# The opening of a one-core attention and mixture-of-experts kernel: the first batch's expert taken from its slots' summed values, one softmax over all its tokens, and W1 loaded between two pieces of the second batch's keys and values

## The chip, the core and the metric

The program runs on one core of a Trainium2 chip. The number that counts is the device time of one execution in microseconds (us). The kernel before takes 393.38 us (median of three executions, 393.33 to 393.97). The engines are named as in the profile: PE is TensorE (PEld its weight loads), DVE is VectorE, ACT is ScalarE, POOL is GpSimd, SP is SyncE. SP only issues transfers here, in order, and each waits for its semaphores at the head of SP's queue.

## What is computed

Two stages follow each other: an attention in which 576 keys and values of each head are first pooled into 32 slots, and a mixture of 8 experts of which each token uses one.

```python
def _attn_ref(q, k, v, phi):              # B, H, S, D = 8, 8, 576, 64; 32 slots
    a = softmax(phi, axis=2)              # over the 32 slots
    k_m = einsum('bhsm,bhsd->bhmd', a, k) # slot keys
    v_m = einsum('bhsm,bhsd->bhmd', a, v) # slot values
    attn = softmax(q @ k_m.T / 8)         # each token over the 32 slots
    return attn @ v_m
def _moe_ref(x, expert_emb, tau, w1, w2): # x: 4608 tokens of 512; 8 experts, hidden 1024
    logits = normed(x) @ normed(expert_emb).T / tau
    e = argmax(logits); gate = softmax(logits)[e]
    return gate * (relu(x @ w1[e]) @ w2[e])
```

The router's logits are linear in the attention's output but for a factor per token, and the output is a mean of slot values, so a token's expert can be read from slot values times the expert embedding.

## The kernel before

A batch of 576 tokens is one stage of eight. The chosen expert's W1 and W2 are loaded once for a batch, and all tokens of the batch are run through it. Tokens that belong to another expert are handled by a loop after the eight batches (`rest`), which runs once for each pair of batch and other expert that `flags` marks; for the drawn inputs no pair is marked.

In a batch, `slots` pools keys and values (matmuls of eT and kx, kl), `scale`, `keys` and `values` make slot keys kT and slot values vT, `score` multiplies kT with the queries (tr, ts), `squares` multiplies vT with vT and with the router's columns (tl), `products` copies that to vv, `fill`, `weigh`, `divide` and `turn` make the softmax of each token (x, then aw), `project` multiplies vT with W1 (pg, then the pair gh and gl), `pairs` multiplies aw with vv (po), and `first` and `second` are the two large layers (ph, py), which use a value and its remainder (gh and gl, aT's two halves, wh and wl).

The order of every engine's instructions is that of the Python calls (the schedule is manual). From batch 0's `first` on, small steps of the next batch are hung into lists that run between the matmul groups of the large layers (`steps`). Before that lies the opening, in `moe_linformer`, lines 1088 to 1167, and the first lines of `batch` (940 to 949): nothing of a large layer can run there. It does batch 0 up to its softmax and the slots, keys and values of batch 1.

In the opening the expert of batch 0 comes from its first 64 tokens: `score` of 64 columns, `fill` and `weigh` of these, `turn`, then `early` (line 123, two matmuls), `best` and `count` (lines 202 and 203) and the two DVE operations of `choose`. SP reads the number (line 220) and issues the two halves of W1 (line 468). The other 512 tokens have a softmax of their own (`others`). Matmuls of a constant (`warm`, line 418) fill PE's idle stretches; their result is not used. For batch 1 all keys and values have been issued on SP before SP waits for the expert.

PSUM is given out in two rings, `pt` (tags t0 to t3) and `mm` (m0 to m3); batch 1's slot sums lie in t3 and m3.

Of the kernel before, what the change touches and what calls it, by code (L numbers as in the profile page):

```python
# [8 lines left out]
F32 = mybir.dt.float32  # L9
F32R = mybir.dt.float32r  # L10
BF16 = mybir.dt.bfloat16
I32 = mybir.dt.int32
# [35 lines left out]
class Tokens:  # L48
# [69 lines left out]

    def early(self, po, to):

        k, nc = self.k, self.nc
        for g in range(NG):
            nc.tensor.matmul(po[to, 144 * g : 144 * g + P + E], lhsT=k.aw[:, g, to], rhs=k.vv[:, g], start=True, stop=True)
        e = po[to].rearrange("p (g m) -> p g m", g=NG)[..., D : D + E]
        nc.vector.tensor_reduce(out=self.lg[to, 0], in_=e.rearrange("p g e -> p e g"), axis=AX.X, op=ALU.add)
        self.best(0, to=to)

    def open(self):
# [70 lines left out]

    def count(self, key, to):  # L200

        self.nc.tensor.matmul(key, lhsT=self.k.ones, rhs=self.k.eb, start=True, stop=False)
        self.nc.tensor.matmul(key, lhsT=self.k.ones[to], rhs=self.oh[to, 0], start=False, stop=True)
        return key

    def choose(self, to=None):

        k, nc, b = self.k, self.nc, self.b
        if b:
            self.key = self.all = key = self.all_at_once()  # L210
        else:
            key = self.pt([P, 512], "key")
            self.spare, key = key[:, E:], key[:, :E]
            self.key = self.all = self.count(key, to)
# [6 lines left out]
        k.load_w1(e, b == 0)  # L221
        return e
# [3 lines left out]

    def kept(self):
        self.held = self.k.wk.tile([P, E], F32, tag="held", name="held")
        self.nc.scalar.copy(self.held, self.key)

    def owner(self):
        k, nc, b = self.k, self.nc, self.b
        cm = k.wk.tile([P, 1], F32, tag="cm", name=f"cm{b}")
        self.own = k.wk.tile([P, E], F32, tag="own", name=f"own{b}")
        key = self.key if b else self.held
        nc.vector.tensor_reduce(out=cm, in_=key, axis=AX.X, op=ALU.max)
        nc.vector.tensor_scalar(out=self.own, in0=key, scalar1=cm, scalar2=None, op0=ALU.is_equal)

    def flags(self):

        self.nc.vector.scalar_tensor_tensor(
            out=self.k.fl[:, self.b], in0=self.all, scalar=float(E), in1=self.own, op0=ALU.is_ge, op1=ALU.subtract
        )
# [44 lines left out]
class Kernel:  # L288
# [64 lines left out]
    def consts(self):  # L353
        nc, st = self.nc, self.st.tile
        self.ident = st([P, P], F32, name="ident")
        make_identity(nc, self.ident)
        self.i8 = st([P, E], F32, name="i8")
        nc.gpsimd.iota(self.i8, pattern=[[1, E]], base=0, channel_multiplier=0, allow_small_or_imprecise_dtypes=True)
        self.rev8 = st([P, E], F32, name="rev8")
        nc.vector.tensor_scalar(out=self.rev8, in0=self.i8, scalar1=-1.0, scalar2=float(E), op0=ALU.mult, op1=ALU.add)  # L360

        self.oh = [st([P, NT + 1, E], BF16, name=f"oh{i}") for i in range(2)]
        self.eb = self.oh[0][:, NT]
        for oh in self.oh:
            nc.vector.tensor_scalar(out=oh[:, NT], in0=self.i8, scalar1=1.0 / (E * P), scalar2=None, op0=ALU.mult)
        nc.vector.memset(self.vv, 0.0)
        nc.gpsimd.memset(self.z2, 0.0)
        self.half = st([P, 1], F32, name="half")
        nc.vector.memset(self.half, 0.5)
# [65 lines left out]

    def load_kv(self, b):
        if 1 < b < B:
            for g in range(NG):
                to, x = self.kl[64 * g : 64 * g + 64], self.kvt[b, :, 4 * g : 4 * g + 4]
                self.nc.sync.dma_start(to, x)  # L440
        if b < B:
            for k in range(4):
                self.nc.sync.dma_start(self.kx[k], self.kv[b, :, k])
                if b < 2 and k == 1:
                    x = self.kvt[b].rearrange("t (g j) d -> (t g) (j d)", g=NG)
                    self.nc.sync.dma_start(self.kl.rearrange("p j d -> p (j d)"), x)

    def load_q(self, b, halves=(0, 1)):
# [14 lines left out]

    def load_w1(self, e, halves=False):

        for k in range(2 if halves else 4):
            c, f = (slice(NC), slice(512 * k, 512 * k + 512)) if halves else (slice(k, k + 1), slice(FF))
            self.nc.sync.dma_start(self.w1s[:, c, f], self.w1[bass.ds(e, 1), :, c, f].rearrange("a p c f -> (a p) c f"))
# [32 lines left out]

    def shares(self, b, gs=range(NG), v=None):

        v = v or self.nc.vector
        nm, sm, rs = self.room(b)
        for g in gs:
            for j in range(4) if g else (None,):
# [3 lines left out]
                )  # L511
        g = slice(gs[0], gs[-1] + 1)
        self.nc.vector.reciprocal(out=rs[:, g], in_=rs[:, g])
# [212 lines left out]

    def project(self, n, vT, room=None):

        nc = self.nc
        for k in range(2):  # L730
            f = slice(512 * k, 512 * k + 512)
            ps = [(room or self.mm)([P, 512], f"pg{n}_{k}{g}") for g in range(NG)]
            for g, j, r, c, i in self.heads():
                nc.tensor.matmul(ps[g][j], lhsT=vT[r, g, c % 2, i], rhs=self.w1s[r, c, f], start=True, stop=True)
            for g in range(NG):
# [66 lines left out]
    def steps(self, b, t, u):  # L802
# [7 lines left out]
        if not b:  # L810
# [114 lines left out]
    def batch(self, b, t, u):  # L925
# [7 lines left out]

        project = self.project(b, self.vT[b % 2]) if u else ()
        if b:
            list(project)
            if u:
                self.scores(b + 1)
        else:
            self.keys(1, lambda *a: self.mm(*a, 3))  # L940
            self.values(1, copy=self.nc.scalar.copy, room=lambda *a: self.mm(*a, 2))
            self.part(0, slice(0, HS), self.nc.scalar.copy)
            next(project)
            self.part(1, slice(0, HS), self.nc.scalar.copy)
            self.second_part = project
            t.attend()
# [136 lines left out]
def moe_linformer(ctx, tc, phiT, qT, kv, kvt, emb, tau, w1, w2, out):  # L1083
# [5 lines left out]
    k.warm(8)  # L1089
    k.warm(25, hot=k.mm([P, 64], "cool", 0))  # L1090
    k.load_phi(0)
# [28 lines left out]
    k.again()  # L1120
    k.load_kv(1)
    k.keys(0)
    k.values(0, copy=k.nc.scalar.copy)
    first, others, few = slice(0, 2), slice(2, BL), slice(0, 64)
    ts = [k.mm([P, 64], f"ts0_{g}", 1 + g) for g in range(NG)]
    k.score(0, ts, 0, 64)
    t.fill(range(NG), first, ts)
    ts = [k.mm([P, S - 64], f"tr0_{g}", g) for g in range(NG)]
    tl = [k.pt([P, D + E], f"tl0_{g}") for g in range(NG)]
    k.score(0, ts, 64, S, (0,))  # L1130
    k.squares(0, tl)
    k.score(0, ts, 64, S, (1,))
    list(t.weigh(range(NG), first))
    k.products(0)
    t.turn(range(NG), first)
    k.largest(1, 0)
    k.softmax(1, (0,))
    t.early(k.mm([P, NC * (D + E)], "po0", 2), few)
    e = t.choose(few)
    k.largest(1, 1)  # L1140
    k.softmax(1, (1,))
    k.load_q(1, (0,))
    k.turn(1, 0)
    k.warm(7, hot=t.spare)
    k.turn(1, 1)
    k.turns += 1
    k.tails(1)
    t.fill(range(NG), others, ts)
    weights = [t.weigh((g,), others) for g in range(NG)]
    for g in range(NG):  # L1150
        next(weights[g])
    for g in range(NG):
        next(weights[g])
        list(weights[g])
    k.shares(1, v=k.nc.gpsimd)
    t.kept()
    for ks in ((0,), (1,), (4,), (2,), (3,)):
        k.slots(1, accs, ks=ks, first=0 in ks, last=3 in ks)
    k.tags = 4
    k.scale(1)  # L1160
    k.again(k.nc.scalar.copy)
    t.divide(range(NG), slice(0, BL), True)
    t.turn(range(NG), slice(0, BL))
    k.load_w2(e)
    k.load_q(1, (1,))
    k.load_phi(2)
    k.warm(3)
    for b in range(B):
# [33 lines left out]
```

## Time and profile before

| | us |
|---|---|
| median of the runs | 393.38 |
| profiled execution | 395.79 |
| its span | 394.0 |
| PE busy | 384.9 (98%) |
| DVE, ACT, POOL busy | 244.3, 214.0, 188.6 |
| first matmul of the large layers (line 753) starts at | 32.59 |

The profile is of one execution; its span is what the trace covers, and 1.8 us of its time lie outside. Times in the trace are counted from the span's start. A row of the timeline has start, length, engine, line and operation, tile written <- tiles read, the shape, how many instructions it merges, and in brackets how long the engine sat idle before and what ended that. PEclk is the granted clock of TensorE as a share of 2.4 GHz; 0.50 is 1.2 GHz. The queue of the SP engine carries nearly all loads (81 of 91 MB).

### The profile page before, as it was taken

How to read it: one execution, taken by the hardware profiler on the slowest of the kernel's cores; microseconds unless marked ns; L12 is line 12 of the kernel's file. 1: busy time of each engine (PE TensorE's matmuls, PEld its weight loads, DVE VectorE, ACT ScalarE, POOL GpSimd, SP SyncE). 2: the span in 40 equal slices, each digit the busy share in tenths (PEclk: the TensorE clock that was granted, in tenths of full speed). 3: DMA queues.
4: the chain of work that ended last, by engine and by line, in shares of the span. 5: the costliest groups of instructions: out<-in, count | busy, mean ns of one | idle time of the engine just before them, and what ended most of it. 6: DMA issues, size and time to landing. Idle time of an engine off the chain costs nothing. (4 is left out here: it accounts for less than half of the span.)

```text
span 394.0 us, 10319 instructions
## 1 busy us (share of the span) xinstructions
PE 384.9 (98%) x3837; PEld 311.1 (79%) x3837; DVE 244.3 (62%) x806; ACT 214.0 (54%) x666; POOL 188.6 (48%) x230
## 2 busy tenths in 40 slices
PE   8799999999999999999999999999999999999995
PEld 5357978889787987879787997879788897879883
DVE  5388895769672798448971798627961596535000
ACT  5257643777585685657665775667642651145011
POOL 1036951588142941559152961549342781529300
PEclk9779999999999999999999999999999999999999
DMA  8979938996779936997479925997279305980011
GB/s 277 393 287 366 356 108 202 318 393 242 160 210 394 399 90 145 326 374 308 86 233 360 402 92 111 342 385 275 60 212 359 120 2 106 296 348 0 30 53 43
DMA packets 68534, 91.24 MB, mean 232 GB/s; under 512 B 40984, under 2 KB 46616, under 8 KB 68352
## 3 DMA queue, kind: packets, MB, share of 16 engines
q1 hardware_dynamic: 65104, 81.02, 61.4%
q0 software_dynamic: 2688, 8.26, 5.8%
q10 hardware_dynamic: 688, 1.26, 1.2%
q8 instruction: 31, 0.51, 0.6%
q14 instruction: 23, 0.19, 0.2%
HBM read 71.19 MB, written 19.33 MB: 230 GB/s over the span
## 5 line engine op out<-in xcount | busy, mean ns | idle before, releaser
L753 PE MATMUL ph<-aT,gh 128*128 128x288 f32 x512 | 103.1, 297 | 0.0
L793 PE MATMUL py<-wh,hh 128*128 128x512 f32 x256 | 100.8, 394 | 0.0
L793 PE MATMUL py<-wl,hh 128*128 128x512 f32 x256 | 99.8, 390 | 0.0
L793 PE MATMUL py<-wh,hl 128*128 128x512 f32 x256 | 99.7, 389 | 0.0
L724 POOL TENSOR_TENSOR wl<-w2s,wh 128x512 fp32r<-128x512 f32 x64 | 83.2, 1300 | 5.1
L753 PEld LDWEIGHTS ph<-aT,gh 128*128 128x128 f32 x512 | 81.8, 188 | 1.8 <-DVE hl L760 0.8
L753 PE MATMUL ph<-aT,gl 128*128 128x288 f32 x256 | 75.4, 294 | 0.0
L757 ACT ACTIVATE hh<-ph 128x224 fp32r<-128x224 f32 (+1 forms) x128 | 48.8, 388 | 33.6 <-PE ph L753 33.0
L760 DVE SCALAR_TENSOR_TENSOR hl<-ph,hh 128x224 fp32r<-128x224 f32 (+1 forms) x128 | 51.8, 417 | 23.5 <-ACT hh L757 16.9
L798 ACT ACTIVATE ys<-py,gate 128x512 f32<-128x512 f32 (+1 forms) x40 | 25.8, 644 | 62.9 <-PE py L793 33.1
L969 POOL DMA_DIRECT2D out_dram<-ys x28 | 16.2, 580 | 90.4 <-ACT ys L798 90.3
L793 PEld LDWEIGHTS py<-wh,hh 128*128 128x128 f32 x256 | 48.1, 188 | 11.0 <-issue 1.4
L793 PEld LDWEIGHTS py<-wh,hl 128*128 128x128 f32 x256 | 48.1, 188 | 10.2
L793 PEld LDWEIGHTS py<-wl,hh 128*128 128x128 f32 x256 | 48.1, 188 | 9.4
L753 PEld LDWEIGHTS ph<-aT,gl 128*128 128x128 f32 x256 | 48.0, 188 | 0.0
L737 DVE TENSOR_TENSOR gl<-pg,gh 128x512 fp32r<-128x512 f32 x32 | 20.0, 684 | 42.0 <-ACT gh L736 42.0
L723 POOL CAST wh<-w2s 128x512 fp32r<-128x512 f32 x62 | 41.3, 666 | 0.1
L714 POOL TENSOR_TENSOR aT<-aw,aT 128x576 fp32r<-128x576 f32 (+1 forms) x18 | 23.5, 1318 | 33.6 <-DVE aT L713 30.2
L553 ACT COPY eT<-xt 32x256 f32<-32x256 f32 x80 | 32.3, 403 | 1.4
L782 PE MATMUL py<-w2s,h 128*64 128x256 f32 x256 | 29.4, 382 | 0.0
L625 ACT COPY kv<-kt 32x64 f32<-32x64 f32 x96 | 23.3, 243 | 6.3 <-DVE kt L615 5.1
L782 PEld LDWEIGHTS py<-w2s,h 128*64 128x64 f32 x256 | 17.7, 137 | 10.7 <-DVE aw L100 2.1
(174 smaller groups left out, 473.4 us busy)
## 6 DMA issues: line engine op xcount, KB each, us to landing
kx<-kv SPq DMA_DIRECT2D x32, 512.0 KB, 10.2
w2s<-w SPq DMA_DIRECT2D x28, 512.0 KB, 9.6
w1s<-w SPq DMA_DIRECT2D x28, 512.0 KB, 6.5
out_dram<-ys POOLq DMA_DIRECT2D x28, 256.0 KB, 6.4
qt<-qT SPq DMA_DIRECT2D x12, 576.0 KB, 9.2
ad<-aw SPq DMA_DIRECT2D x8, 576.0 KB, 10.4
td<-x SPq DMA_DIRECT2D x56, 72.0 KB, 2.4
ea<-td SPq DMA_DIRECT2D x7, 512.0 KB, 4.2
```

The lines of the kernel that those rows point to most:

```text
L553: nc.scalar.copy(eT[to, :8, m].rearrange("p (g k) m -> p g k m", g=NG), xt[at, :, q : BL - 2 : 4])
L625: nc.scalar.copy(y, self.kt[32 * l : 32 * l + 32, g, h + 2 * i :: 2 - 4 * i])
L714: self.nc.gpsimd.tensor_tensor(out=al, in0=a, in1=ah.bitcast(F32), op=ALU.subtract)
L723: (copy or self.nc.scalar.copy)(h, x)
L724: self.nc.gpsimd.tensor_tensor(out=l, in0=x, in1=h.bitcast(F32), op=ALU.subtract)
L737: nc.vector.tensor_tensor(out=self.gl[:, g, f], in0=ps[g], in1=self.gh[:, g, f].bitcast(F32), op=ALU.subtract)
L753: nc.tensor.matmul(p, lhsT=w[:, g, fs], rhs=x[:, g, to], start=g == 0 and k == 0, stop=g == 1 and k == 2)
L757: nc.scalar.activation(self.hh[:, f, at], q, AF.Relu)
L760: nc.vector.scalar_tensor_tensor(out=self.hl[:, f, at], in0=q, scalar=0.0, in1=self.hh[:, f, at].bitcast(F32), op0=ALU.max, op1=ALU.subtract)
L782: nc.tensor.matmul(p[64 * j : 64 * j + 64], lhsT=self.h4[:, f], rhs=self.w2s[:, f, d * j : d * j + d], start=f == 0, stop=f == 7,)
L793: nc.tensor.matmul(p, lhsT=h[:, f, to], rhs=w[:, f], start=f == 0 and k == 0, stop=f == 7 and k == 2)
L798: nc.scalar.activation(y[:, :d], p, AF.Copy, scale=gate[:, i : i + 1])
```

## The change

- Guess: `early`, `count` and the 64-token path go. `guess` sums the router's columns of vv over all slots with two matmuls by a matrix of ones; `pick` takes the largest of the eight sums and its place with MAX, MAX_INDEX and an AND on DVE; `kept` goes, and `owner` compares with the number itself.
- One softmax: batch 0 has one `weigh` of 576 tokens for each half g, in two matmul groups (448 or 512 columns and 64), with `fill` of the one half between the slots' work of batch 1.
- Loads: q comes in two halves of 576 KB, not in three pieces (256, 448, 448 KB). SP issues two of batch 1's four kx pieces, then waits for the expert, issues W1's first half, then kl and the other two kx pieces, then W1's second half.
- Order on PE: W1's first half is multiplied (`project`, first half) before batch 1's slots; batch 1's `keys` and `values` move from the opening into batch 0's `first` (after groups 5 and 6). `warm` counts: 25, 7, 3 before; 29, 14, 2, 3 after.

The diff, cut to what is spoken of:

```diff
+    def guess(self):
+        key = self.pt([P, 512], "key")
+        self.spare, self.key = key[:, E:], key[:, :E]
+        for g in range(NG):
+            nc.tensor.matmul(self.key, lhsT=k.all1, rhs=k.vv[:, g, D : D + E], start=not g, stop=g == NG - 1)
+    def pick(self):
+        nc.vector.max(out=top, in_=self.key)
+        nc.vector.max_index(out=at, in_max=top, in_values=self.key)
+        nc.vector.tensor_scalar(out=self.at, in0=at[:, :1].bitcast(I32), scalar1=E - 1, scalar2=None, op0=ALU.bitwise_and)
+        return nc.sync.value_load(self.at[:1], min_val=0, max_val=E - 1)
...
-        if not b:
-            for c, f in ((slice(4), slice(P)), (slice(2), slice(P, S)), (slice(2, 4), slice(P, S))):
-                self.nc.sync.dma_start(self.qt[:, c, f], self.qT[0, :, c, f])
-        elif b < B:
+        if b < B:
...
+            first[5].append(lambda: self.keys(1, self.mm))
+            first[6].append(lambda: self.values(1, copy=self.nc.scalar.copy, room=self.mm))
...
-    k.load_kv(1)
+    k.load_kv(1, (0, 1))
     k.keys(0)
-    k.values(0, copy=k.nc.scalar.copy)
...
+    scores(0)
     tl = [k.pt([P, D + E], f"tl0_{g}") for g in range(NG)]
     k.squares(0, tl)
     k.products(0)
+    t.guess()
+    te.append(k.pt([P, 64], "te0_1"))
+    scores(1)
+    work = [t.weigh((g,), all) for g in range(NG)]
+    t.fill((0,), slice(2, BL), tr)
+    t.fill((0,), slice(0, 2), te)
+    e = t.pick()
+    k.load_w1(e, 0)
+    k.load_kv(1, (2, 3))
+    k.load_w1(e, 1)
     k.load_q(1, (0,))
+    k.warm(14, hot=t.spare)
+    list(work[0])
+    for g in range(NG):
+        k.largest(1, g)
+        k.softmax(1, (g,))
     k.turn(1, 0)
+    k.warm(2, at=2)
+    t.fill((1,), slice(2, BL), tr)
+    t.fill((1,), slice(0, 2), te)
+    list(work[1])
     k.turn(1, 1)
     k.tails(1)
+    k.shares(1, v=k.nc.gpsimd, invert=False)
+    project = k.project(0, k.vT[0], apart=True)
+    next(project)
+    t.divide(range(NG), all, True)
+    t.turn(range(NG), all)
+    k.invert(1)
+    next(project)
+    for g in range(NG):
+        k.part(g, slice(0, HS), k.nc.scalar.copy)
     for ks in ((0,), (1,), (4,), (2,), (3,)):
         k.slots(1, accs, ks=ks, first=0 in ks, last=3 in ks)
```

On PE, from batch 0's slot values (tv) to the expert's number; tr and ts are scores, tl the squares, po the early output, key the sums. Before:

```order
L636 MATMUL tv_0_306<-ident,ks 128x128 x2
L654 MATMUL ts_0_313<-qt,kv_80 32x64 x4
L654 MATMUL ts_1_314<-qt,kv_80 32x64 x4
L654 MATMUL tr_0_325<-qt,kv_80 32x512 x4
L662 MATMUL tl_0_327<-kv_80 32x72 x4
L662 MATMUL tl_1_328<-kv_80 32x72 x4
L654 MATMUL tr_1_326<-qt,kv_80 32x512 x4
L123 MATMUL po_361<-vv,aw 64x136 x2
L202 MATMUL key<-oh_165,ones 128x8
L203 MATMUL key<-oh_165,ones 128x8
L519 MATMUL te_0_388<-ident,ex 128x128 x4
```

And after the change, the same place:

```order
L637 MATMUL tv_0_307<-ident,ks 128x128 x2
L655 MATMUL tr_0_314<-qt,kv_80 32x512 x4
L655 MATMUL te_0_316<-qt,kv_80 32x64 x4
L663 MATMUL tl_0_325<-kv_80 32x72 x4
L663 MATMUL tl_1_326<-kv_80 32x72 x4
L197 MATMUL key<-vv,h_97 128x8 x2
L655 MATMUL tr_1_315<-qt,kv_80 32x512 x4
L655 MATMUL te_1_342<-qt,kv_80 32x64 x4
```

The sums stand ahead of the second scores now, and behind them only the copies to vv; the scores of 64 columns (ts) are no longer ahead of everything that needs the large part of q.

On SP, from batch 1's first transfers of keys and values (kx_70, kx_71) to W1 (w1s). Before:

```order
L443 DMA kx_70<-kv 128x1024
L443 DMA kx_71<-kv 128x1024
L446 DMA kl<-kvt 128x512
L443 DMA kx_72<-kv 128x1024
L443 DMA kx_73<-kv 128x1024
L220 TENSOR_LOAD seli
L468 DMA w1s<-w 128x4x512
L468 DMA w1s<-w 128x4x512
```

After:

```order
L445 DMA kx_70<-kv 128x1024
L445 DMA kx_71<-kv 128x1024
L208 TENSOR_LOAD ai
L464 DMA w1s<-w 128x4x512
L444 DMA kl<-kvt 128x512
L445 DMA kx_72<-kv 128x1024
L445 DMA kx_73<-kv 128x1024
L464 DMA w1s<-w 128x4x512
```

Three transfers of batch 1 (1.25 MB) now stand behind the expert's number and behind half of W1.

On ACT, after the exponentials of batch 1's phi; eT and kt are copies of transposes, x is batch 0's softmax, gh the copy of `project`, aT the rounded weights, ks the scaled slots. Before:

```order
L520 COPY eT<-te_1_401 128x512
L527 COPY kt<-tz_407 128x256
L76 ACTIVATE x<-x 128x512 x2
L229 COPY held<-key 128x8
L593 ACTIVATE ks<-acc0t,rs_357 128x128
L593 ACTIVATE ks<-acc0m,rs_357 128x128
L630 COPY ks<-ks 128x2x64
```

After:

```order
L521 COPY eT<-te_0_401 128x512
L76 ACTIVATE x<-x 128x576
L521 COPY eT<-te_1_416 128x512
L528 COPY kt<-tz_422 128x256
L739 CAST gh<-pg_00_431 128x512
L739 CAST gh<-pg_01_432 128x512
L714 CAST aT_86<-aw 128x288 x2
L594 ACTIVATE ks<-acc0t,rs_394 128x128
L594 ACTIVATE ks<-acc0m,rs_394 128x128
```

The second exponential of the tokens now stands behind the copy of te_0, and the scaling of the slots behind the two casts of aw, which need the turned softmax.

## Rows read from the trace of the kernel before

**Rows 1.** The page, part 1: busy time, share of the span, instructions.
```profile
PE 384.9 (98%) x3837; PEld 311.1 (79%) x3837; DVE 244.3 (62%) x806; ACT 214.0 (54%) x666; POOL 188.6 (48%) x230
```
**Rows 2.** Stretches: length, busy time of PE, PEld, DVE, ACT, POOL, PEclk, DMA share, GB/s.
```profile
14.00:15.00 1.00, 0.00 (x0) 0.00 (x0) 0.82 (x4) 0.51 (x4) 0.00 (x0) 0.60 1.07 404
21.00:22.00 1.00, 1.00 (x5) 0.55 (x4) 1.00 (x2) 0.42 (x1) 0.00 (x0) 0.50 0.13 53
24.00:25.00 1.00, 1.00 (x8) 0.73 (x6) 1.00 (x2) 0.00 (x0) 1.00 (x1) 0.78 1.05 383
32.00:48.00 16.00, 16.00 (x170) 14.19 (x167) 13.90 (x55) 10.83 (x34) 12.78 (x16) 1.00 1.03 366
```
**Rows 3.** The timeline of PE in the opening, 13 to 33 us.
```profile
13.14 0.41 PE L636 MATMUL tv<-ident,ks 128*128 128x128 f32 x2
...
15.31 1.08 PE L654 MATMUL tr<-qt,kv 64*32 64x512 f32 x4 [1.49 <-DMA qt<-qT]
...
16.13 1.45 PE L654 MATMUL tr<-qt,kv 64*32 64x512 f32 x8
...
18.53 1.14 PE L123 MATMUL po<-vv,aw 128*64 128x136 f32 x4
...
21.30 3.15 PE L418 MATMUL key<-ones 128*128 128x504 bf16 x7
24.24 0.70 PE L519 MATMUL te<-ident,ex 128*128 128x128 f32 x4
...
28.46 0.40 PE L601 MATMUL tk<-ident,ks 128*128 128x128 f32 x2
...
29.12 1.09 PE L734 MATMUL pg<-w1s,kv 64*32 64x512 f32 x16
...
31.17 0.86 PE L140 MATMUL po<-vv,aw 64*64 64x72 f32 x40 [0.16 <-DVE aw L98]
31.96 0.88 PE L172 MATMUL tt<-ident,aw 128*128 128x128 f32 x6
32.59 0.51 PE L753 MATMUL ph<-aT,gh 128*128 128x288 f32 x2
```
**Rows 4.** The transfers of SP: the timeline, 3 to 24 us.
```profile
3.99 1.96 SPq L451 DMA_DIRECT2D qt<-qT  x3
...
12.47 3.09 SPq L443 DMA_DIRECT2D kx<-kv  x2
21.86 1.35 SPq L468 DMA_DIRECT2D w1s<-w  x2
```
**Rows 5.** SP's own waits, 0 to 60 us: in total, times, longest.
```profile
SPq L443 <- DMA qt<-qT: 2.8, 2, 2.4
```
**Rows 6.** Line 468, W1's two halves: from issue to landing.
```profile
DMA to landing us min/median/max: 5.1/6.7/8.3
```
**Rows 7.** The timeline of DVE in the opening.
```profile
17.63 0.47 DVE L698 COPY vv<-tl 64x72 f32<-64x72 f32 x2 [2.74 <-PE tl L662]
...
20.69 0.14 DVE L217 TENSOR_SCALAR seli<-ki 1x1 int32<-1x1 int32 x1
...
22.65 1.22 DVE L72 TENSOR_REDUCE mx<-x 128x16 f32<-128x512 f32 x2
...
26.46 1.41 DVE L85 TENSOR_REDUCE z<-x 128x18 f32<-128x576 f32 x2 [1.11 <-ACT x L76]
...
29.32 0.78 DVE L98 STREAM_TRANSPOSE aw<-x 128x576 f32<-128x576 f32 x1
```
**Rows 8.** The timeline of ACT in the opening.
```profile
21.57 0.77 ACT L498 ACTIVATE ex<-ex,nm 128x576 f32<-128x576 f32 x1 [1.48 <-issue]
...
25.78 1.16 ACT L76 ACTIVATE x<-x 128x512 f32<-128x512 f32 x2
...
27.70 0.37 ACT L593 ACTIVATE ks<-acc0t,rs 128x128 f32<-128x128 f32 x1 [0.70 <-PE acc0t L576]
```
**Rows 9.** The timeline of POOL, 28 to 30 us.
```profile
28.67 1.63 POOL L90 TENSOR_TENSOR x<-x,z 128x576 f32<-128x576 f32 x1 [3.52 <-DVE z L87]
```

More of the change, by code (lines that the diff above doesn't have):

```diff
@@ L117, in attend @@
         self.pairs()
[L119 to L126, printed above, removed]
     def open(self):
@@ L198, in all_at_once, with choose @@
         return key
[L200 to L206, printed above, removed]
-        k, nc, b = self.k, self.nc, self.b
[L209 to L214, printed above, removed]
+    def guess(self):
+        k, nc = self.k, self.nc
+        key = self.pt([P, 512], "key")
[3 more added lines that the diff above has]
+    def pick(self):
+        k, nc = self.k, self.nc
+        top = k.wk.tile([P, E], F32, tag="top", name="top")
+        at = k.wk.tile([P, E], mybir.dt.uint32, tag="at", name="at")
+        self.at = k.wk.tile([P, 1], I32, tag="ai", name="ai")
+        nc.vector.max(out=top, in_=self.key)
+        nc.vector.max_index(out=at, in_max=top, in_values=self.key)
+        nc.vector.tensor_scalar(out=self.at, in0=at[:, :1].bitcast(I32), scalar1=E - 1, scalar2=None, op0=ALU.bitwise_and)
+        return nc.sync.value_load(self.at[:1], min_val=0, max_val=E - 1)
+    def choose(self):
+        k, nc, b = self.k, self.nc, self.b
+        self.key = self.all = key = self.all_at_once()
         ki = k.wk.tile([1, 1], I32, tag="ki", name=f"ki{b}")
@@ L234, in owner @@
         self.own = k.wk.tile([P, E], F32, tag="own", name=f"own{b}")
-        key = self.key if b else self.held
-        nc.vector.tensor_reduce(out=cm, in_=key, axis=AX.X, op=ALU.max)
-        nc.vector.tensor_scalar(out=self.own, in0=key, scalar1=cm, scalar2=None, op0=ALU.is_equal)
+        if b:
+            nc.vector.tensor_reduce(out=cm, in_=self.key, axis=AX.X, op=ALU.max)
+        else:
+            nc.vector.tensor_copy(out=cm, in_=self.at[:, :1])
+        nc.vector.tensor_scalar(out=self.own, in0=self.key if b else k.i8, scalar1=cm, scalar2=None, op0=ALU.is_equal)
     def flags(self):
         self.nc.vector.scalar_tensor_tensor(
-            out=self.k.fl[:, self.b], in0=self.all, scalar=float(E), in1=self.own, op0=ALU.is_ge, op1=ALU.subtract
+            out=self.k.fl[:, self.b], in0=self.all, scalar=float(E), in1=self.own, op0=ALU.is_ge, op1=ALU.is_gt
         )
@@ L367, in consts @@
         nc.gpsimd.memset(self.z2, 0.0)
+        self.all1 = self.h4[:, :2].rearrange("p f t -> p (f t)")
+        nc.gpsimd.memset(self.all1, 1.0)
         self.half = st([P, 1], F32, name="half")
@@ L462, in q, with load_w1 @@
         return self.sT[:, c] if c < 2 else self.x[:, c - 2].rearrange("p k m -> p (k m)")
-    def load_w1(self, e, halves=False):
-        for k in range(2 if halves else 4):
-            c, f = (slice(NC), slice(512 * k, 512 * k + 512)) if halves else (slice(k, k + 1), slice(FF))
+    def load_w1(self, e, half=None):
+        for k in range(4) if half is None else (half,):
+            c, f = (slice(k, k + 1), slice(FF)) if half is None else (slice(NC), slice(512 * k, 512 * k + 512))
             self.nc.sync.dma_start(self.w1s[:, c, f], self.w1[bass.ds(e, 1), :, c, f].rearrange("a p c f -> (a p) c f"))
@@ L511, in shares, with invert @@
                 )
-        g = slice(gs[0], gs[-1] + 1)
+        if invert:
+            self.invert(b, gs)
+    def invert(self, b, gs=range(NG)):
+        rs, g = self.room(b)[2], slice(gs[0], gs[-1] + 1)
         self.nc.vector.reciprocal(out=rs[:, g], in_=rs[:, g])
@@ L734, in project @@
                 nc.tensor.matmul(ps[g][j], lhsT=vT[r, g, c % 2, i], rhs=self.w1s[r, c, f], start=True, stop=True)
+            if apart and not k:
+                yield
             for g in range(NG):
@@ L932, in must @@
                 self.split_w()
[L934 removed]
         if b:
[L936 removed]
+            list(self.project(b, self.vT[b % 2]) if u else ())
             if u:
@@ L939, in batch @@
         else:
[L940 to L945, printed above, removed]
             t.attend()
@@ L1089, in moe_linformer @@
     k.warm(8)
-    k.warm(25, hot=k.mm([P, 64], "cool", 0))
+    k.warm(29, hot=k.mm([P, 64], "cool", 0))
     k.load_phi(0)
@@ L1120, in moe_linformer @@
     k.again()
-    k.load_kv(1)
+    k.load_kv(1, (0, 1))
     k.keys(0)
-    k.values(0, copy=k.nc.scalar.copy)
[L1124 to L1128, printed above, removed]
+    k.values(0)
+    all, tr, te = slice(0, BL), [k.mm([P, S - 64], f"tr0_{g}", g) for g in range(NG)], [k.mm([P, 64], "te0_0", 2)]
@@ L1129, in moe_linformer, with scores @@
+    def scores(g):
+        k.score(0, tr, 64, S, (g,))
+        k.score(0, te, 0, 64, (g,))
+    scores(0)
     tl = [k.pt([P, D + E], f"tl0_{g}") for g in range(NG)]
-    k.score(0, ts, 64, S, (0,))
     k.squares(0, tl)
-    k.score(0, ts, 64, S, (1,))
-    list(t.weigh(range(NG), first))
     k.products(0)
[L1135 to L1141, printed above, removed]
@@ L1157, in moe_linformer @@
+    next(project)
[3 more added lines that the diff above has]
+    next(project)
+    for g in range(NG):
+        k.part(g, slice(0, HS), k.nc.scalar.copy)
     for ks in ((0,), (1,), (4,), (2,), (3,)):
         k.slots(1, accs, ks=ks, first=0 in ks, last=3 in ks)
-    k.tags = 4
+        if ks == (1,):
+            k.warm(3, at=2)
+    k.tags, k.turns = 4, 3
     k.scale(1)
     k.again(k.nc.scalar.copy)
-    t.divide(range(NG), slice(0, BL), True)
-    t.turn(range(NG), slice(0, BL))
@@ L1166, in moe_linformer @@
     k.load_phi(2)
-    k.warm(3)
+    k.second_part = project
     for b in range(B):
```

27 lines of the change are left out of this document (7 added, 20 removed).

## The prediction

> **What bounds the kernel.** I read the page first: PE is busy for 98% of the span [rows 1]. The stretches say where it isn't. From 32 us on PE is busy without a pause (16.00 of 16.00 us) at its full 2.4 GHz [rows 2], so from the first matmul of the large layers at 32.59 us [rows 3] the end follows by PE work alone, and the change is worth what it moves that start, plus or minus the PE work that it puts behind it. The opening is read from the timelines of PE, DVE, ACT and SP, one beside the other.
>
> The reader is to see three things there. First, PE waits 1.49 us for the large part of q and starts the long scores (tr) at 15.31 [rows 3]. Second, the granted clock falls at about 14.2 us (the mean from 14 to 15 is 0.60 of full speed) and is back at about 24.4 (mean 0.78 from 24 to 25) [rows 2], at the end of 3.15 us of constant matmuls [rows 3]; everything between runs at 1.2 GHz. Third, the expert is known at 20.83 (20.69 + 0.14) [rows 7], W1 is issued at 21.86 [rows 4] and its first half lands 5.1 us later, at 26.96 [rows 6]; in between the transfers have nothing to do (53 GB/s from 21 to 22) [rows 2].
>
> **The change part by part.** *Start of the long scores.* q's first piece had landed by 12.4: of the 2.8 us that SP's kx transfers wait for q, 0.4 belong to the first, issued at 12.47 [rows 4, 5]. The second piece landed by 15.31. The first half of q is 320 KB longer than the first piece. At 404 GB/s [rows 2] that is 0.8 us, so 13.25; drawn in proportion of bytes between the two landings (320 of 448 KB of 2.9 us) it is 14.5. I take 13.9. The scores need only kT, and slot values (tv) are done on PE at 13.55 [rows 3], so they start at 13.9, with a gap of 0.35 us on PE in place of 1.49.
>
> *The clock.* This is the term that decides. Forecast: with long scores in the place of the gap the clock holds at 2.4 GHz. Against it: the fall at about 14.2 comes only some 0.4 us after the small scores ended, so what went before has its part in it, and that stays, less 0.34 us of small scores. I price both cases.
>
> A rule weighed here: the Trainium skill (TensorE: Matmul & The Clock Gate, "Why this matters for your kernels") has TensorE throttled by long idle stretches between bursts of matmuls. The trace differs: the clock fell early in a gap of 1.49 us [rows 2, 3]. By the page the kernel before would not have been slowed and the change would save no clock; by the trace short work with gaps is enough, and that raises the chance of the slow case below.
>
> *Expert, at 2.4 GHz.* From the long scores' first pass to the copies of the squares it took 17.63 - 15.31 = 2.32 us at 1.2 GHz [rows 3, 7]: half is 1.15, and 0.1 for the 64 columns now between: copies at 15.15, done (0.47) at 15.62. The two matmuls of the guess: the nearest row is line 123, also two such matmuls, 1.14 us at 1.2 GHz [rows 3]. Bounds 0.2 to 1.14; I take 0.5: 16.15. DVE meanwhile transposes the scores (0.78 for 576 columns [rows 7], two pieces, 0.95) until 16.6 and then does MAX, MAX_INDEX and the AND. No trace shows the first two. The smallest row near, the AND before the number, is 0.14, and a pass over 576 columns, the other end, is 0.71 (1.41 for two) [rows 7]; eight columns are nearer to the first, with a step to the next operation I take 0.2 each: 17.2. SP takes 21.86 - 20.83 = 1.03 us from the number to the issue: W1 at 18.2, landed at 18.2 + 5.1 = 23.3, that is 3.6 us earlier.
>
> The Trainium skill (Vector Engine (DVE) Microarchitecture Reference, 3.9) makes the search for an index two operations, a load of the values sought and the search. By that the number is 0.2 us later, W1 lands at 23.5 and the sum below loses 0.2; no run shows it yet.
>
> *Softmax of all tokens.* DVE goes on with largest and difference of the first half (0.7 each; 512 columns take 0.61 [rows 7]): 18.6; the two maxima of phi, 1.4: 20.0. ACT's first exponential of phi starts with the first maximum (19.3) and ends at 20.2 with its sum (0.77 and 0.1) [rows 8]. On PE the second scores end at about 17.5 (q's second half lands not later than the third piece did, by about 16.4), then 14 constant matmuls at half of 0.43 us (seven in 3.15 [rows 3], less the last one's tail): 3.0, so 20.5, just behind ACT. Transposing te_0 there hides nothing else. DVE: scores of the second half 0.95, largest and difference 1.4: 22.35. ACT: exponential 0.65 (1.16 for two of 512 [rows 8]): 23.0, behind the copy of te_0 that ended at 21.75. Sum 0.7, reciprocal and start of POOL's product 0.8 (28.67 - 27.87) [rows 7, 9]: 24.5. POOL's product 1.63: 26.15. Turning on DVE, 1.0 with the tail piece: 27.15. Before, this stood at 31.2 (the pairs waited for it until 31.17 [rows 3]), so 4.0 us are won on DVE.
>
> *Behind it.* ACT's order puts cast (0.43) and scaling (0.37 [rows 8]) behind the turn, and the pairs of the third token block write the bank that the scaling reads: they start at 28.0. By then 66 of 80 pair matmuls are left (14 fill other banks first): 66 x 0.0215 = 1.42 [rows 3], and 0.63 from the transposes to the large layers (32.59 - 31.96): 30.05. That is 2.54 earlier than 32.59. W1 doesn't bind: half of it lands at 23.3, its matmuls take 1.09 us; kl and the two kx pieces behind it (1.31 MB at 383 GB/s [rows 2]) land 3.4 later, at 26.7, and the last slots (0.45) are done at 27.2, 0.8 before the pairs go on. That is the cover of everything on SP, the three transfers behind the wait for the expert among them. W1's second half and W2 follow some 2 us later than the first; POOL and PE ask for them only in the large layers.
>
> *Work moved behind the start.* keys and values of batch 1 took PE from 28.46 to 29.12: 0.66 us [rows 3], now inside the large layers, in full. Their ACT copies lie beside PE work of 2.4 us for three groups, nearly full. Removed rows of DVE (early's four, the small softmax) and of ACT are in the above. Four more constant matmuls at 4.4 us and a memset on POOL lie in idle time.
>
> **Sum**: -2.54 + 0.66 = -1.88 us. The profiled execution (395.79) would take 393.9; the median, 2.4 lower than it, 391.5.
>
> **Rivals.** *A: the clock falls as before and the warm-up becomes the bound (slower).* Scores from 13.9 at 1.2 GHz: copies at 16.4, done at 16.9, guess 1.14: 18.05, number at 18.65, W1 at 19.7, landed 24.8. The second scores take two passes (0.82 and 1.08 [rows 3]) and 0.2 for the 64 columns: 20.15. Then the 14 constant matmuls: seven at 0.43 before the clock is back, as in the row at 21.30, seven at 0.215: 24.65. Only then te_0 (0.7), its copy on ACT (0.6), and behind that copy the second exponential (0.65), sum and reciprocal 1.5, POOL 1.63, turn 1.0, cast and scaling 0.8, 1.42 and 0.63: 33.6. That is +1.0 and with 0.66 +1.65: 395.0; with scores from 15.0, 396.1. For it: the stretch ahead of the fall has little more work than before. Against: the gap in which it falls is filled. It decides from the point at which te_0 starts later than 23.0 (32.59 - 0.66 - 8.9).
>
> *B: the clock falls, but the second scores and the first constant matmuls bring it back at about 20 us (no change).* Then the 14 take 3.0 and end at 23.15, and the large layers start 8.93 later at 32.1: -0.5 + 0.66 = +0.2, 393.6.
>
> *C: the change doesn't do what it says: a wrong guess.* Each wrong expert costs a pass of about 45 us ((394.0 - 32.59) / 8). By the reference all 576 tokens of the first batch use one expert, and the sum of its slot values points to the same: next to nothing.
>
> *D: q's half comes late, but the clock holds.* Scores from 15.0: all of DVE's chain 0.35 to 1.1 later: 391.9 to 392.6. This is in the forecast's own range, 390.8 to 392.6; its low end is scores from 13.55 with a shorter pick and a scaling that the pairs don't wait for.
>
> **Chances.** Forecast with D 0.60, A 0.25, B 0.13, C and the rest 0.02. The time is that of the forecast. The range takes the forecast's end below and goes to 395.2 above, which holds B and the nearer part of A. About 0.2% (0.8 us) is what a measurement of this kernel tells from no change: faster 0.63 (nearly all of the forecast and a little of B), same 0.12, slower 0.25.
>
> **What would show it.** Right: a granted clock of 1.00 from 4 us to the end, long scores before 14.5, W1 issued before 19 and landed before 24, the pairs before 29, line 753's counterpart at about 30. A granted clock of 0.50 behind 14 us with te_0 behind 23 us shows A. Wrong on the small terms: MAX and MAX_INDEX far over 0.2 us, a pause of the transfers that makes the last slots later than the turn, or PE gaps in batch 0's large layers where keys and values stand now.

## The result: slower by 0.8%, where faster was forecast

After the change the kernel takes 396.80 us (median of 7, 395.21 to 398.73); before it took 393.38 in the same job (7 runs, 391.77 to 393.97). The ratio is 1.0079 with an interval of 1.0058 to 1.0100. The forecast was 391.5, its range ended at 395.2, and 0.63 stood on faster. Both kernels were run and profiled once more, 396.43 against 393.39 (12 and 25 runs, 1.0079 again, 1.0054 to 1.0103), and these four profiles hold most of the answer:

| us | before | before again | after | after again |
|---|---|---|---|---|
| profiled execution | 395.79 | 392.77 | 395.26 | 398.54 |
| its span | 394.0 | 391.0 | 393.4 | 396.7 |
| mean granted clock | 0.986 | 0.999 | 0.998 | 0.995 |
| large layers start at | 32.59 | 29.64 | 30.84 | 34.59 |
| span behind that start | 361.4 | 361.4 | 362.6 | 362.1 |

The page after, part 1, answers [rows 1]: PE works as long as before, so nothing is to be found in totals.

```profile
PE 384.1 (98%) x3848; PEld 311.3 (79%) x3848; DVE 244.4 (62%) x803; ACT 213.1 (54%) x662; POOL 188.3 (48%) x231
```

The stretches after, columns as in [rows 2]:

```profile
14.00:15.00 1.00, 1.00 (x32) 0.50 (x24) 0.45 (x2) 0.18 (x2) 0.00 (x0) 1.00 1.04 407
24.00:25.00 1.00, 1.00 (x36) 0.71 (x32) 0.97 (x2) 0.61 (x2) 0.60 (x1) 1.00 1.05 233
32.00:48.00 16.00, 15.61 (x163) 13.57 (x161) 12.35 (x44) 11.32 (x40) 13.66 (x17) 1.00 1.04 369
```

The clock is whole (1.00, the 2.4 GHz level), as forecast. The transfers move 233 GB/s from 24 to 25 us with their engines full, and PE has 0.39 us of pause in the large layers, where it had none. From 18 to 20 us they stand nearly still; before again the slowest 2 us between 12 us and the large layers, 20 to 22, are at 290 GB/s (first row after, second before again):

```profile
18.00:20.00 2.00, 2.00 (x11) 0.86 (x9) 2.00 (x4) 1.50 (x4) 0.00 (x0) 1.00 0.19 46
20.00:22.00 2.00, 1.95 (x18) 0.97 (x16) 2.00 (x4) 1.79 (x5) 0.94 (x5) 1.00 0.79 290
```

The timeline of PE after, answering [rows 3]:

```profile
13.61 1.06 PE L655 MATMUL tr<-qt,kv 64*32 64x512 f32 x8
...
15.47 0.61 PE L197 MATMUL key<-vv,h 128*128 128x8 f32 x4 [0.42 <-ACT vv L701]
...
17.12 3.15 PE L417 MATMUL key<-ones 128*128 128x504 bf16 x14
20.10 0.66 PE L520 MATMUL te<-ident,ex 128*128 128x128 f32 x4
...
23.26 1.09 PE L735 MATMUL pg<-w1s,kv 64*32 64x512 f32 x16 [1.42 <-DMA w1s<-w]
...
26.93 0.43 PE L577 MATMUL acc0t<-kx,eT 128*32 128x128 f32 x8 [0.22 <-DMA kx<-kv]
...
28.21 0.43 PE L577 MATMUL acc0t<-kx,eT 128*32 128x128 f32 x8 [0.65 <-DMA kx<-kv]
...
28.79 1.49 PE L131 MATMUL po<-vv,aw 64*64 64x72 f32 x80
30.21 0.87 PE L163 MATMUL tt<-ident,aw 128*128 128x128 f32 x6
30.84 0.51 PE L756 MATMUL ph<-aT,gh 128*128 128x288 f32 x2
...
39.38 0.53 PE L756 MATMUL ph<-aT,gh 128*128 128x288 f32 x2 [0.39 <-DVE hl L763]
```

Three waits for transfers now stand in the opening: for W1, and for two kx pieces. The pairs (po) follow the last kx without a pause. SP's transfers after [rows 4] show why these are late: kl and two kx pieces are issued behind the number, and until then little else is left to move.

```profile
18.02 0.72 SPq L464 DMA_DIRECT2D w1s<-w  x1
18.84 0.56 SPq L444 DMA_DIRECT2D kl<-kvt  x1
19.50 0.91 SPq L445 DMA_DIRECT2D kx<-kv  x2
20.62 0.57 SPq L464 DMA_DIRECT2D w1s<-w  x1
```

DVE after, from the last squares to the number [rows 7]; the search for the place is two operations:

```profile
16.38 0.14 DVE L205 MAX8 top<-key 128x8 f32<-128x8 f32 x1
16.55 0.09 DVE L206 MATCH_VALUE_LOAD at<-top,key 128x8 f32 x1
16.63 0.17 DVE L206 FIND_INDEX8 at<-top,key 128x8 uint32<-128x8 f32 x1
16.83 0.15 DVE L207 TENSOR_SCALAR ai<-at 128x1 int32<-128x1 int32 x1
```

### The profile page after: what moved, and what is told of

The parts are those of the page before. It is cut to its first block, busy times and chain, and to the rows that moved or that the text cites. A ratio compares the mean times of both kernels' runs of the same rounds, so it can differ in the third digit from the quotient of the medians.

```text
span 393.4 us, 10332 instructions
## 1 busy us (share of the span) xinstructions
PE 384.1 (98%) x3848; PEld 311.3 (79%) x3848; DVE 244.4 (62%) x803; ACT 213.1 (54%) x662; POOL 188.3 (48%) x231
## 5 line engine op out<-in xcount | busy, mean ns | idle before, releaser
L715 POOL TENSOR_TENSOR aT<-aw,aT 128x576 fp32r<-128x576 f32 (+1 forms) x18 | 23.5, 1321 | 35.6 <-DVE aT L714 29.7
L626 ACT COPY kv<-kt 32x64 f32<-32x64 f32 x96 | 23.3, 243 | 6.4 <-DVE kt L616 5.3
```

The lines of the kernel that those rows point to most:

```text
L626: nc.scalar.copy(y, self.kt[32 * l : 32 * l + 32, g, h + 2 * i :: 2 - 4 * i])
L715: self.nc.gpsimd.tensor_tensor(out=al, in0=a, in1=ah.bitcast(F32), op=ALU.subtract)
```

## The experiments

**1. Both kernels again, unchanged.**

> The kernel before once more, for the clocks of its usual executions. Theory (the clock was no gain to be had): the profiled execution of before took 395.79 us at a mean granted clock of 0.986, its median run 393.38; if the usual runs do not have the clock's fall, they show 0.996 or more, and a profile of such a run has the large layers start at about 30.2 (32.59 - 2.4) instead of 32.59, with PEclk 1.0 from 14 to 24 us. Rival: the usual runs have the fall too (0.986) and the 2.4 us lie in transfers that land at other times. Time: 393.4 under both.

Measured: 393.35 (ratio 0.9993, 0.9973 to 1.0014), all twelve runs with a mean clock of 0.997 or more. Of the 25 runs of before in that job, 22 have 0.997 or more; the other three (0.949 to 0.995) are the three slowest, 395.65 to 395.92. Over all jobs, 18 of 125 runs of before have less than 0.997; they take 393.25 to 397.21. The profile that the prediction was read from, 395.79 at 0.986, is of this rarer kind. PE in the profile of before again:

```profile
14.49 1.06 PE L654 MATMUL tr<-qt,kv 64*32 64x512 f32 x8
...
19.15 1.65 PE L418 MATMUL key<-ones 128*128 128x504 bf16 x7
...
26.13 1.09 PE L734 MATMUL pg<-w1s,kv 64*32 64x512 f32 x16 [0.47 <-DMA w1s<-w]
...
28.09 0.98 PE L140 MATMUL po<-vv,aw 64*64 64x72 f32 x48 [0.16 <-issue]
...
29.64 0.51 PE L753 MATMUL ph<-aT,gh 128*128 128x288 f32 x2
```

The same lines as in [rows 3], 2.95 us earlier at the end: no gap ahead of the first long scores (0.58 us ahead of the second), seven constant matmuls in 1.65 us instead of 3.15. The theory holds: the fall of the clock, on which the forecast's gain rested, is not in the usual run. The wait for q is another matter. Of eight profiles of the kernel before and its variants, all with q in three pieces, three have it ahead of the first long scores (1.49 to 1.52 us), and in one of these, `b_kv_layers` of experiment 3, the clock holds (1.00 from 14 to 16 us and in every stretch after it up to the large layers):

```profile
14.00:16.00 2.00, 0.58 (x18) 0.25 (x18) 1.16 (x5) 1.14 (x5) 0.00 (x0) 1.00 1.04 398
...
16.10 0.63 PE L654 MATMUL tr<-qt,kv 64*32 64x512 f32 x4 [1.51 <-DMA qt<-qT]
```

So this gap alone does not always bring the clock down, and filling it does not surely save a fall.

> The kernel after the change once more. Its profiled execution took 395.26, its median run 396.8. Theory (transfers behind the wait for the expert are late): 396.8 again, granted clock 0.996 or more, and if the profile is of a slower run, its extra time is in waits of PE for W1 (1.42 us in the first profile) and for kx (0.22 and 0.65). Rival (clock): extra time is a stretch at 1.2 GHz, mean clock 0.99 or less. Rival (work moved into the large layers): extra PE idle time between 32 and 48 us beyond the 0.39 us there.

Measured: 396.43 (395.02 to 399.28). The profiled execution is one of the longer ones (398.54), and its PE shows the next link:

```profile
24.08 1.09 PE L735 MATMUL pg<-w1s,kv 64*32 64x512 f32 x16 [1.42 <-DMA w1s<-w]
...
30.38 0.43 PE L577 MATMUL acc0t<-kx,eT 128*32 128x128 f32 x8 [2.15 <-DMA kx<-kv]
...
30.95 2.64 PE L131 MATMUL po<-vv,aw 64*64 64x72 f32 x80
33.53 1.30 PE L163 MATMUL tt<-ident,aw 128*128 128x128 f32 x6
34.59 0.51 PE L756 MATMUL ph<-aT,gh 128*128 128x288 f32 x2
```

Here the last kx is 2.17 us later than in the first profile (0.82 of it is there already at W1's product), PE stands still for it, and behind that the clock falls to the 1.2 GHz level (stretches of the same run):

```profile
30.00:31.00 1.00, 0.62 (x20) 0.42 (x20) 0.00 (x0) 0.08 (x1) 0.00 (x0) 1.00 1.05 428
31.00:32.00 1.00, 1.00 (x40) 1.00 (x40) 0.00 (x0) 0.85 (x3) 0.00 (x0) 0.52 1.02 408
```

so that the pairs take 2.64 us instead of 1.49. Both the theory (waits for kx) and the clock rival have a part. The four slowest of the twelve runs (397.69 to 399.28) are the four with a mean clock of 0.994 or 0.995; the other eight lie at 395.02 to 397.08. The third, extra pauses in the large layers, is out.

**2. The loads.** First kl and the two kx pieces ahead of the wait, nothing else:

```diff
-    k.load_kv(1, (0, 1))
+    k.load_kv(1)
...
-    k.load_kv(1, (2, 3))
```

> The changed kernel with all of batch 1's keys and values issued ahead of the wait for the expert, as before; W1's halves follow each other. Theory (the transfers stand still from 17 to 19.5 us because kl and two kx pieces queue behind the wait): W1's first half lands about as early (22.5 to 23.3), PE's waits for kx (0.87 us) go, large layers start 0.7 to 1.0 us earlier than 30.84, time 394.8 to 396.0. Rival (loss is the work moved into the large layers): time within 0.3 us of 396.8. Rival (W1 must be first in the queue): W1 lands 1 us later and it takes 397.5 or more.

Measured: 397.8 (1.0091, 1.0058 to 1.0124). The first theory falls as it stood: W1 was issued at 18.87 and landed 7.5 us later. The time is that of the last rival, though W1 is 2.3 to 3.1 us later than in the two profiles of after, not 1.

```profile
26.38 1.96 PE L735 MATMUL pg<-w1s,kv 64*32 64x512 f32 x16 [3.68 <-DMA w1s<-w]
```

The pieces are no longer late, but W1 is, and in the changed order of PE all slots stand behind its product; after 3.68 us of pause PE goes on at 1.2 GHz. W1's place and PE's order belong together. Hence both undone, with keys and values in the opening, and the guess, the single softmax and its warm-up kept. The order on DVE and ACT goes back with it (the scaling of the slots ahead of the tokens' division, the three constant matmuls behind the slots), so this run does not part the loads from the order:

```diff
+    k.load_kv(1)
...
+    for ks in ((0,), (1,), (4,), (2,), (3,)):
+        k.slots(1, accs, ks=ks, first=0 in ks, last=3 in ks)
...
+    k.keys(1, lambda *a: k.mm(*a, 3))
+    k.values(1, copy=k.nc.scalar.copy, room=lambda *a: k.mm(*a, 2))
+    project = k.project(0, k.vT[0])
```

> The changed kernel with the guess, the single softmax and its warm-up kept, but loads and PE order as before: all of batch 1's keys and values are issued ahead of the wait for the expert, its slots, keys and values stand ahead of W1's first product on PE. Theory (the loss is in the loads put behind the wait and in what PE then waits for; the guess itself wins next to nothing since W1 lands behind the other transfers anyway): W1 issued at about 18.9, landed at about 26.2 as in the profile of before that kept its clock (26.13), large layers start at 29.2 to 29.7 (29.64 there), time 392.8 to 393.6, no PEclk below 1.0. Rival (the later number of DVE operations or the single softmax is the loss): still 395.5 or more.

Measured: 393.77, before 393.09 (1.0021, 1.0006 to 1.0035): 0.7 us over before, where the change was 3.0 to 3.4 over it; the large layers start at 30.21 (0.5 behind the expected 29.2 to 29.7), and no stretch from 12 us on has a clock under 1.00. The other way round, the kernel before with only these loads (two kx, wait, half of W1, kl, two kx, half of W1):

> The kernel before with only the loads of the change: two kx pieces, then the wait for the expert, W1's first half, kl, two kx pieces, W1's second half; its own PE order, expert and softmax. Theory (loads behind the wait are the loss): the wait ends at about 20.1, the last kx lands 9 to 10 us later at 29.5 to 30, the slots, keys, values and W1's product stand behind it, large layers at 33 to 34: 396.5 to 398. Rival (the order of loads costs nothing since the same bytes have to come): 393.4 to 394.

Measured: 400.5 (1.0184, 1.0162 to 1.0205), all six runs with a mean clock of 0.981 to 0.991. The direction is that of the theory; the size (7.4 us) is about twice the expected. In the profile, the slowest of the six (402.95), the clock falls twice: behind a wait of 1.52 us for q (mean 0.76 from 16 to 18 us), and again in a pause of 4.35 us in which PE waits for kl. Stretches of this run around the second:

```profile
26.00:28.00 2.00, 0.00 (x0) 0.00 (x0) 1.89 (x5) 0.65 (x2) 0.01 (x1) 0.82 1.07 376
28.00:30.00 2.00, 0.04 (x3) 0.07 (x5) 1.82 (x5) 0.00 (x0) 1.63 (x1) 0.50 0.89 219
30.00:32.00 2.00, 1.58 (x28) 1.09 (x32) 0.89 (x2) 0.00 (x0) 0.00 (x0) 0.50 1.01 399
```

Put side by side: loads and PE's order both of before, 393.1 to 393.8; the new loads alone 400.5 (in the kernel before), the new order alone 397.8 (in the changed one), both 396.4. Neither alone comes out better than the two together, and the loads alone are far worse.

**3. Keys and values of batch 1.** In the changed kernel back into the opening (the two lines out of `first`, two calls ahead of `attend`):

> The changed kernel with keys and values of batch 1 in the opening again, between the slots and the pairs, as before. Theory (they cost the same 0.66 us of PE in either place, plus the 0.39 us in which PE waits at 38.99 when they are inside the layers): 0 to 0.4 us faster than 396.8. Rival (moving them is the loss): 1.05 us faster, 395.7 or less. Other rival (their ACT copies in the opening delay the pairs): slower than 397.3.

Measured: 396.63, beside 396.43: no difference. In its profile 361.0 us lie behind the start of the large layers, not 362.1 to 362.6; the opening is longer by about as much, since the keys now stand behind the late kx: from the last kx's first product to the large layers it takes 3.96 us (29.60 to 33.56), where it took 2.63 in the first profile of after. And the kernel before with only the move:

> The kernel before with only keys and values of batch 1 moved into the large layers of batch 0. Theory: they cost the large layers 0.7 to 1.1 us (0.66 of PE and a wait of up to 0.4), and win nothing in the opening, where PE waits 0.47 us for W1 behind them: 394.0 to 394.5. Rival (they stand on the path in the opening too): 393.4 to 393.8.

Measured: 394.86, before 393.09 (1.0048, 1.0031 to 1.0066): +1.8, more than expected. 362.6 us lie behind the start (361.4 in both profiles of before), with the pause of the changed kernel:

```profile
39.24 0.54 PE L753 MATMUL ph<-aT,gh 128*128 128x288 f32 x2 [0.41 <-DVE hl L760]
```

That is 1.2 of the 1.8. In this profile (395.14) the large layers also start 1.05 later than before again, behind the wait of 1.51 us for q, and four of its twelve runs have a mean clock of 0.992 to 0.996; the rest may lie there, which was not taken apart. In the version with slots first, moved once more:

> The changed kernel with loads and slots in the order of before, but keys and values of batch 1 inside the large layers, as the change has them. Theory (they cost more there than in the opening: 0.66 us of PE and a wait of 0.4, and the kernel before lost 1.8 by them): 394.4 to 395.3 beside 393.77. Rival (with PE as the bound of the opening they are free to move): 393.4 to 394.0.

Measured: 394.34 (1.0015, 0.9991 to 1.0039) beside 393.77 (1.0021): 0.6 in raw time, just below the theory's range, nothing by the ratios. 362.0 us lie behind its start. Over all profiles, six with the move have 362.0 to 363.0 behind the start and the other eleven 360.9 to 361.4.

**4. The clock in the gap ahead of the last kx.**

```diff
+        if ks == (2,):
+            k.warm(8, at=2)
```

> The changed kernel with eight constant matmuls more (1.7 us) between the slots of the third and the fourth kx piece, where PE stood still for 0.65, 1.08 and 2.15 us. Theory (in the slower part of the runs that gap makes the clock fall, which costs 1 to 2 us more in the pairs): no run with a mean clock under 0.996, the slowest runs (397.7 to 399.3 in 5 of 12) go, the fastest become up to 1 us slower, median 395.8 to 396.6, highest 397.5. Rival (the clock has no part, only the landing of kx): runs as widely spread as without it, median 396.4 to 397.4.

Measured: 397.21 (1.0102, 1.0081 to 1.0122). The runs that were to go are four of twelve, not five. Five of six runs here keep the clock (0.997 or more) and lie within 396.78 to 397.41; the sixth (400.42, 0.991) lost it earlier, behind a pause of 1.35 us for q. The narrow spread is the theory's, the median is the rival's: nothing is won. With six runs, and a profile only of the sixth, it is not shown that the filled gap prevents falls, nor what it costs in the others.

**5. The guess alone, in the kernel before.** Only `guess`, `pick` and what they need:

> The kernel before with only the guess: the expert from the slots' summed values (two matmuls, MAX, MAX_INDEX, AND) in place of the early output of 64 tokens; its own loads, its softmax in two parts, its PE order, its 25, 7 and 3 constant matmuls. Theory (the guess is a gain that the rest of the change gives away): W1 issued at about 18.5 instead of 20.12, landed at 24.5 to 25.2 (its 1 MB behind the last kx), DVE free of the five small operations and their waits, the last turn at 27.0 to 27.6 instead of 28.29, large layers at 28.6 to 29.3: 392.0 to 392.8. Rival (W1 lands behind the other transfers anyway and something else ends last): within 0.3 us of before.

Measured: 397.37 (1.0088). Not the guess was priced here: by the edit the maxima of phi stood behind the number on DVE, PE had nothing for 3.58 us, and the clock fell (0.68 from 18 to 20). The expectation had not seen that.

> The kernel before with only the guess, now with the small softmax where it stood, the two matmuls of the guess ahead of the second half of the long scores, and six constant matmuls behind these so that PE doesn't stand still. Theory (the guess wins W1's issue, but DVE, busy without a pause from the copies of the squares to the last turn, sets the end of the opening): number at 17.6 instead of 19.1, W1 issued 18.6 to 19.0, no fall of the clock, last turn 0.4 to 0.6 earlier than 28.29, large layers 0.2 to 0.6 earlier than 29.64: 392.7 to 393.2. Rival (the guess itself costs something that hasn't been seen): 393.8 or more. Rival (W1's landing was the bound): 392.3 or less.

Measured: 396.63 (1.0077, 1.0063 to 1.0092), again not the guess. The constant matmuls were written ahead of the search and share its tile, and the search waited for them:

```profile
19.04 0.17 DVE L205 MAX8 top<-key 128x8 f32<-128x8 f32 x1 [2.80 <-PE key L417]
```

With the search written first:

```diff
-    k.warm(6, hot=t.spare)
     t.turn(range(NG), first)
     e = t.pick()
     k.load_w1(e, True)
+    k.warm(7, hot=t.spare)
     k.largest(1, 0)
```

> The kernel before with only the guess; the search on DVE now stands ahead of the seven constant matmuls that fill PE behind the second half of the long scores, so it waits only for the two matmuls of the guess. Theory (DVE sets the end): number at 17.5 instead of 19.1, W1 issued 18.5 to 18.8, last turn 27.6 to 28.1 instead of 28.29, large layers 29.1 to 29.6 instead of 29.64, clock without a fall: 392.7 to 393.4. Rival (the early number is a gain of 1 us or more that the change gave away): 392.3 or less. Rival (a hidden cost of the guess): 393.9 or more.

Measured: 392.65, before 393.81 (0.9977, 0.9957 to 0.9997). W1 is issued at 18.66, 1.5 us earlier than at 20.12, the last turn ends at 28.20 and the large layers start at 29.55: as the theory has it, by a gain at the edge of what can be told. Against before again (28.29 and 29.64) the profile is 0.09 us ahead, and it is that much ahead already at the slots' transposes (13.14 against 13.23): the early number itself moved nothing there.

> As b_guess3, without the seven constant matmuls between the two turns of batch 1 (PE's 1.65 us there held up the second turn, ACT's copy of it and the exponentials of the scores behind that copy, for which DVE waited 0.62 us). Theory (DVE's chain sets the end of the opening): DVE no longer waits before the sums, last turn at about 27.5 instead of 28.20, large layers at 28.9 instead of 29.5, time 391.9 to 392.5 beside 392.65. Rival (W1's landing ends last, its first product can't start before about 26): 392.5 to 392.8. Rival (PE's gap makes the clock fall): 394 or more with a mean clock under 0.996.

Measured: 393.10 (0.9999, 0.9976 to 1.0022). DVE's last turn did come 0.91 us earlier (27.29), and nothing was won: now W1 is last, the rival's mechanism, at a time a little over the rival's.

```profile
26.44 1.09 PE L733 MATMUL pg<-w1s,kv 64*32 64x512 f32 x16 [0.78 <-DMA w1s<-w]
27.47 1.48 PE L131 MATMUL po<-vv,aw 64*64 64x72 f32 x80
28.88 0.88 PE L163 MATMUL tt<-ident,aw 128*128 128x128 f32 x6
```

W1 issued at 18.47 is there at 26.44; issued at 20.12, in before again, at 26.13. In `b_guess3` it is issued at 18.66 and lands 7.3 us later, in `b_guess2` at 20.70 and 5.2 us later, both at about 26. With all of batch 1 ahead of it in the queue its landing does not follow its issue.

**6. A version that keeps what helps.** As the version with slots first, `k.turn(1, 1)` and `k.tails(1)` moved ahead of `list(work[1])`:

> As the changed kernel with its slots first, and with the turn of batch 1's second half of phi ahead of the second exponential of the scores in ACT's order (PE stood 1.14 us for that copy). Theory: slots end at 24.6 instead of 25.85, W1's first product stands at its landing, large layers up to 0.8 us earlier: 393.0 to 393.5 beside 393.77 without it. Rival (the turn of the tokens on DVE or W1's landing ends last): 393.6 to 393.9.

> The changed kernel with loads and slots in the order of before and the turn of phi ahead of the second exponential, once more. Theory (no gain that can be measured): 392.6 to 393.4, its interval against before holds 1. Rival (a small gain): 392.9 or less with an interval below 1.

Measured: 392.91 (0.9988, 0.9960 to 1.0017), and again 392.80 against 393.81 (0.9968, 0.9951 to 0.9984). PE's pause for the copy went from 1.14 to 0.15 us. The second interval lies below 1, the first holds it: a gain of 0.1 to 0.3% at best. With loads and order of before, the guess and the one softmax in this form, or the guess alone in `b_guess3`, are worth that much.

## Why the prediction was wrong

Forecast 391.5, measured 396.4 to 396.8: 5.1 us. The steps in their order:

**The sum's base failed first.** "The profiled execution (395.79) would take 393.9; the median, 2.4 lower than it, 391.5." The 2.4 are for the most part the clock's fall, which the usual run of before doesn't have (experiment 1); the same wait for q without a fall, in `b_kv_layers`, starts the large layers 1.05 later than before again, where the first profile starts them 2.95 later. The sum took the fall out once as a gain of the change (the clock that holds), and once more in going to the median. Against a start at 29.64, the forecast's 30.05 and its 0.66 are a loss of 1.07, that is about 394.4: the prediction's own numbers said slower, on the right base. The difference of 2.4 us between profile and runs stood there to be asked about, together with a mean clock of 0.986.

**The cover of the transfers failed next** ("the last slots (0.45) are done at 27.2, 0.8 before the pairs go on"), and the number in it was the last kx: 26.7 forecast, 28.21 in the profile, 30.38 in the other. The 1.31 MB behind W1's half were put at 383 GB/s and 3.4 us; they took 4.95 (23.26 to 28.21), and from 24 to 25 us moved at 233. The cover of 0.8 us became the wait. Up to there the steps are good: long scores 13.61 (13.9), vv copied at 15.57 (15.62), number at 16.98 (17.2), W1 issued at 18.02 (18.2), landed at 23.26 (23.3), te_0 at 20.10 (20.5). The last turn was forecast at 27.15 and ends at 26.97. The search took two operations, 0.25 us together (16.55 to 16.80), where one was put at 0.2. The Trainium skill (Vector Engine (DVE) Microarchitecture Reference, 3.9) has it as two operations; the trace agrees. With the last kx late, all 80 pairs start at 28.79, where the last 66 were to go on at 28.0, and the large layers start at 30.84 instead of 30.05: 0.79.

**The 0.66 us for keys and values "inside the large layers, in full" were too small**: 1.2 behind the start in the profile (362.6 against 361.4). 0.66 are matmuls, 0.39 a pause that the trace ends with DVE's hl (the prediction had ACT's copies in view, "nearly full"), and the rest (0.15) is not located: 0.54 more than the forecast in all.

These three are 2.4 + 0.79 + 0.54 = 3.7, which leads from 391.5 to after's profiled run. The other 1.3 lie between after's profiled run (395.26, near the low end of its seven) and its median: the second profile has the last kx 2.2 us later and a fall of the clock behind the pause in front of it, and four of twelve runs have a mean clock as low as that one's. Rival A had slower by the clock, at another place and for another reason; that its times, 395.0 to 396.1, come near the measured one is luck. No rival had the kx pieces as the bound, but the last lines of the prediction name last slots later than the turn, and PE gaps in the large layers, as signs of being wrong: both came. That W1's early issue is worth little where batch 1's loads stand ahead of it (experiments 2 and 5) was not in the prediction either: it priced W1's landing as issue plus 5.1 us, which fits where the queue has run dry at the issue (18.02 to 23.26 after), not where batch 1 is still ahead (7.5 us in `a_kx_first`).

The Trainium skill (TensorE: Matmul & The Clock Gate, "Why this matters for your kernels"), which the prediction weighed against the trace, warns of long pauses of PE between bursts. The runs take its side in kind: each fall in the opening that a profile shows comes in or behind a pause of PE (1.35 to 4.35 us). The length alone doesn't decide: 1.42 us in the first profile of after, 1.51 us in `b_kv_layers` and 2.34 us in `b_guess2` went without one. The prediction's own reading of the trace, that short work with gaps is enough, fails on `b_kv_layers`, where the same wait for q left the clock whole; what decides stays open.

## What to carry to other kernels

Before a profile's stalls are priced, hold its own time and mean clock against the runs: where it is slower than the median, the stall that looks worth removing may be the rare event that made it so, and it must not be counted as gain and as correction both. A load that is put behind a wait in an in-order queue is priced by everything that has to pass between that wait and its use, and its consumer's place in the engine's order has to move with it. Where PE has no other work, a late transfer costs more than its delay, because the clock can fall in the pause and stay down for what follows (pairs of 2.64 us instead of 1.49).

## What the runs showed of the hardware that was not expected

- The kx pieces moved slowly right behind W1's half: 233 GB/s from 24 to 25 us with the DMA engines full (share 1.05); kx pieces issued ahead of the wait in the kernel before ran, together with kl, at 398 to 406 GB/s (16 to 20 us of before again). It shows in the second profile too (225 GB/s, 24 to 26, share 0.95). The cause was not found.
- An operation on DVE that reads one part of a PSUM tile waited 2.80 us for matmuls that write another part of it (`b_guess2`); whether the program's semaphores or the memory ask for that, the trace doesn't tell.
- Landings differ by 1.5 to 2 us from run to run: the same q piece was waited for 1.5 us (before, and two of its variants) or not at all (before again), and the last kx of the changed kernel was there at 28.21 or 30.38.
